# Query products of the head over 128 tokens at once instead of two tiles of 64

## The chip, the cores and the metric

The kernel runs on one core of a Trainium2 chip. The metric is the device time of one execution in microseconds (us), lower is better. Five engines work beside each other, each on its own list of instructions in order: TensorE (PE; the profile shows its weight loads as a row of their own, PEld), VectorE (DVE), ScalarE (ACT), GpSimd (POOL), and SyncE (SP), which here only issues DMAs.

## The reference

Two blocks follow each other. The first is a linear attention with a feature map of degree two: with `a = x S1^T` and `b = x S2^T` (8 values each), a token's 64 features are all products `a_i b_j`.

```python
q_p, k_p = phi(q), phi(k)                  # (b, h, s, 64)
kv  = einsum('bhsf,bhsd->bhfd', k_p, v)
z   = sum(k_p, axis=2)
num = einsum('bhsf,bhfd->bhsd', q_p, kv)
den = einsum('bhsf,bhf->bhs', q_p, z)[..., None] + 1e-6
x   = (num / den)                          # -> (4352, 128)
h   = x @ w_in                             # 128 -> 2048
out = where(h > 0, h, exp(min(h, 0)) - 1) @ w_out
```

q, k and v are (4, 4, 1088, 32) (batches, heads, tokens, width), in fp32. S1, S2 and the two weights arrive as 64-bit floats and are rounded to fp32 on the chip. All products are in fp32.

## The kernel before, in words

**Tiles.** A batch has 17 half tiles of 64 tokens (`NT`). The four heads of 32 make 128 partitions: `qT[b]` is (128, 17, 64), heads and widths down, half tiles and tokens along. All 68 half tiles are cut into 9 groups of 8 (512 tokens; the last has 4). `half_tile(g, k)` gives batch and half tile of the k-th of group g.

**Stages.** The head, up to about 15.6 us, computes the keys' features of batch 0 and from them `kv` and `z`, and then the queries of groups 0 and 1. After it the second block runs over the steps (group, pair of 128 columns of `w_in`): `mm1` makes `h`, ScalarE and VectorE apply the activation, `mm2` multiplies by `w_out`. For groups from 2 on a scheme with seven products instead of eight takes the place of `mm2`. Attention of later batches and groups is put between these steps.

**Order.** Nothing is scheduled by a planner: the order of calls in the code (lines 952 to 1006 for the head, then the loop of line 1107) is each engine's order of work. Waits on data are semaphores.

**TensorE tiles.** A product may use a part of the array's columns: `tile_position=(0, 64 * u)` puts a stationary operand of 64 columns in the left or right half, and two such products can stand side by side; 32 columns make four. The profile prints this form as 128*64 or 128*32, and the full array as 128*128. An fp32 product is recorded as two weight loads and two matmuls (a transpose as one of each).

**The steps that the change touches**, in the order of TensorE's list:

- `Z_first` (line 472): `z_tile` sums products of the keys' values over the tokens into `zps`; ScalarE copies the result to `zl` (line 441).
- `q1_first` (line 511): queries of group 0 times `Sab` (both sketches, 64 columns), into `abqp`. The queries are the stationary operand, in eight tiles of 64 tokens. ScalarE copies to `abq` (line 520).
- `Z` (line 444): `SXh` stationary, `zl` moving (32 columns), into columns 96 to 127 of `zps`, in two tiles of 64 for batch 0. `quarters` (line 254) cuts the stationary operand into tiles. VectorE masks the result into the third part of `SW` (`Z_out`, line 450): sketch and z folded into one matrix over the widths. Later batches call `Z` too, with the width that `width[0]` holds, and aren't touched.
- `keep_warm(1, 96, 64)` (line 261): products of ones that nothing reads, 96 columns in two tiles of 64.
- `q1z_first` (line 523): queries of group 0 times the z part of `SW` (32 columns), into `zqp`. VectorE multiplies it with `abq` into `pw` (line 603), sums (`den`, 608), takes the reciprocal (609), scales `a` (`an`, 611) and forms the 64 features per head (`qp`, 624, in two halves). Two weight roundings (`RA`, line 101) are put between.
- `KA(0)` (line 428) and `KS_first` (481): `kv` of batch 0 and its transpose `kvS`.
- `q4_early(0)` (line 636): eight transposes of `qp`; ScalarE copies to `qpT` (637).
- `q1_second` (line 532): queries of group 1 times all of `SW` (96 columns), into `abwp`. ScalarE copies to `abw` (541). It also waits for VectorE's transpose of the second part of `qT` (281).
- `q5_early(0)` (line 643): `kvS` times `qpT`, into `xps`; ScalarE copies to `xg` (649). With it the first `mm1` starts (`h`, line 257).

Of the kernel before, what the change touches and what calls it, by code (L numbers as in the profile page):

```python
# [27 lines left out]
def kernel(  # L28
# [21 lines left out]
    nc = tc.nc  # L50
    B, H, S, D = q.shape
    R = S1.shape[0]
    P = 128
# [19 lines left out]
    qT = [const.tile([FD, NT, 64], F32, name=f"qT{b}") for b in range(2)] * 2  # L73
# [180 lines left out]
    def quarters(dst, lhs, rhs, tile=None, **kw):  # L254
        tile = tile or width[0]
        for c in range(0, P, tile):
            nc.tensor.matmul(dst[c:c + tile], lhs[:, c:c + tile], rhs, skip_group_check=True,  # L257
                             tile_position=(0, c), **kw)


    def keep_warm(n, cols=256, tile=P):
        ones = nc.const_aps.tensor(1.0, [P, 256], F32)
        for i in range(n):
            for c in range(0, P, tile):
                nc.tensor.matmul(idle[c:c + tile, :cols], ones[:, :tile], ones[:, :cols], skip_group_check=True,  # L265
                                 tile_position=(0, c))
# [17 lines left out]
    SXh = const.tile([P, FD], F32, name="SXh")  # L284
# [10 lines left out]
    Sab = const.tile([FD, H, 2 * R], F32, name="Sab")  # L295
    SW = const.tile([FD, H, 3, R], F32, name="SW")
# [109 lines left out]
    def KO_first(t0, t1):  # L406
        half, o = divmod(t0, 5)
        n = t1 - t0
        a_ = kf_ps[half][:, 64 * o:64 * (o + n)].rearrange("p (m x r) -> p m x r", x=2, r=R)[:, :, 1, :]
        b_ = feats[0][:, 0, t0:t1].rearrange("p t h r -> p (t h) r")  # L410
        nc.vector.tensor_mul(feats[0, half][:, o:o + n].rearrange("p t h i j -> p (t h) i j"),
                             _ap(a_, list(a_.ap[1:]) + [[0, R]]), _ap(b_, [[R, n * H], [0, R], [1, R]]))
# [30 lines left out]

    def Z(b, ps, zl):

        quarters(ps[:, 96:128], SXh[:], zl[:], None if b else 64)

    def Z_out(b, ps):
        z = wzs[b] = SW[:, :, 2, :] if b == 0 else work.tile([FD, H, R], F32, name="wz", tag="wz")[:]
# [22 lines left out]
    def Z_first():  # L472
        ps = psum.tile([P, 512], F32, name="zps", tag="h", bufs=4)
        for i in range(KT):
            z_tile(0, ps, i)
        return ps, ZC(0, ps)
# [21 lines left out]
    def half_tile(g, k):  # L498
        return divmod(8 * g + k, NT)
# [11 lines left out]
    def q1_first():  # L511
        p = psum.tile([P, 512], F32, name="abqp", tag="aux")
        for i in range(4):
            for u in range(2):
                b, t = half_tile(0, 2 * i + u)
                nc.tensor.matmul(p[64 * u:64 * u + 64, i * 64:i * 64 + 64], qT[b][:, t, :],
                                 Sab[:].rearrange("p h y -> p (h y)"),
                                 skip_group_check=True, tile_position=(0, 64 * u))
        abw[0] = work.tile([P, H * 4, 2 * R], F32, name="abq", tag="abq", bufs=1)
        nc.scalar.copy(abw[0][:].rearrange("p (h t) y -> p h t y", h=H),  # L520
                       p[:, :256].rearrange("p (t h y) -> p h t y", t=4, h=H))

    def q1z_first():
        p = psum.tile([P, 512], F32, name="zqp", tag="h", bufs=4)
        for i in range(4):
            for u in range(2):
                b, t = half_tile(0, 2 * i + u)
                nc.tensor.matmul(p[64 * u:64 * u + 64, i * 32:i * 32 + 32].rearrange("p (h r) -> p h r", h=H),
                                 qT[b][:, t, :], SW[:, :, 2, :], skip_group_check=True, tile_position=(0, 64 * u))
        return p[:, :128].rearrange("p (t h r) -> p h t r", t=4, h=H)  # L530

    def q1_second():
        p = psum.tile([P, 512], F32, name="abwp", tag="h", bufs=4)
        for i in range(4):
            for u in range(2):
                b, t = half_tile(1, 2 * i + u)
                nc.tensor.matmul(p[64 * u:64 * u + 64, i * 96:i * 96 + 96], qT[b][:, t, :],
                                 SW[:].rearrange("p h x r -> p (h x r)"), skip_group_check=True,
                                 tile_position=(0, 64 * u))
        abw[1] = work.tile([P, H * 4, 3 * R], F32, name="abw1", tag="abq1", bufs=1)  # L540
        nc.scalar.copy(abw[1][:].rearrange("p (h t) y -> p h t y", h=H),
                       p[:, :384].rearrange("p (t h y) -> p h t y", t=4, h=H))
# [412 lines left out]
    transp(qT, "q", 0, 0, 8)  # L955
    zps, zl = Z_first()
    q1_first()
    KO_pool()
    KO_first(4, 5)
    KO_first(5, 7)  # L960
    Z(0, zps, zl)
    Z_out(0, zps)
    KO_first(7, KT)
    keep_warm(1, 96, 64)
    zq = q1z_first()
    q2_den(0, zq, lambda: RA(0))
    q2_out(0, 2, lambda: RA(1))
# [8 lines left out]
    RE(0)  # L976
    RE(1)
    q1_second()
    q5_early(0)
    keep_warm(1, 192, width[0])  # L980
# [62 lines left out]
    def turn(b):  # L1043
        Z(b, kv_ps[b], zls.pop(b))
        KV(b, kv_ps[b])
# [157 lines left out]
```

## Time and profile before

| | |
|---|---|
| median of 3 runs | 265.75 us (265.44 to 265.97) |
| profiled execution | 265.08 us, its span 263.3 us |
| PE busy | 257.8 us (98%), 4127 matmuls |
| PEld busy | 160.5 us (61%), 4127 loads |
| DVE, ACT, POOL busy | 188.2, 184.5, 168.2 us |
| granted TensorE clock | 1.0 (the mean over the span) |
| loads and matmuls of `abqp`, `zqp`, `abwp` | 16 each |
| loads and matmuls of `zps` in `Z` | 4 |

The span is the part of the execution that the trace covers. A row of the timeline has start and duration in us, engine, line, operation, output<-inputs, the form of the tile and the number of instructions merged into the row. Its duration runs from the start of the first to the end of the last. A matmul's record is longer than the time for which it holds the array, since matmuls are pipelined: the distance of two starts says more of the pace than one record's length.

### The profile page before, as it was taken

To read this page: it belongs to the slowest core of one execution; us is meant where nothing else is said; L and a number is where in the kernel's file an instruction comes from. 1 tells how busy PE (TensorE), PEld (TensorE's weight loads), DVE (VectorE), ACT (ScalarE), POOL (GpSimd) and SP (SyncE) were. 2 spreads that over 40 slices of the span, in tenths; PEclk is the share of its full clock that TensorE was granted. 3 is DMA by queue.
4 is the path that set the end of the run, shared out by engine and by line. 5 is a ranking of instruction groups with operands and counts; after the bars stand their busy time and mean duration, and the time that the engine had idled before them with its cause. 6 is when DMAs were issued, how large, how long until landed. Compare 5 with 4: busy or idle time off the path is not lost.

```text
span 263.3 us, 9739 instructions
## 1 busy us (share of the span) xinstructions
PE 257.8 (98%) x4127; PEld 160.5 (61%) x4127; DVE 188.2 (71%) x349; ACT 184.5 (70%) x356; POOL 168.2 (64%) x251
## 2 busy tenths in 40 slices
PE   8899999999999999999999999999999999999994
PEld 7652334354346756667666666665666666667994
DVE  6899999997969997996477676644446445674651
ACT  2479978677567656775587777776777777777793
POOL 4400009105477996798869799888688888998300
PEclk9999999999999999999999999999999999999999
DMA  5997099020011110000100110011001100110011
GB/s 176 339 349 209 2 277 230 1 72 18 2 24 26 26 20 2 2 4 17 31 3 0 29 18 0 2 19 25 3 2 21 23 4 0 18 20 8 2 30 32
DMA packets 26442, 13.73 MB, mean 52 GB/s; under 512 B 19328, under 2 KB 24576, under 8 KB 26400
## 3 DMA queue, kind: packets, MB, share of 16 engines
q1 hardware_dynamic: 25968, 12.76, 18.9%
q8 instruction: 32, 0.52, 0.9%
q10 hardware_dynamic: 368, 0.30, 0.3%
q0 software_dynamic: 64, 0.07, 0.1%
q14 instruction: 10, 0.08, 0.1%
HBM read 10.88 MB, written 2.23 MB: 50 GB/s over the span
## 4 chain that ended last, share of the span: by engine, by line
PE 96%; POOL 1%; DVE 1%; ACT 1%; issue 0%
PE h L257 44%; PE pb L792 16%; PE pa L792 13%; PE o L257 5%; PE pb L768 4%; PE ol L257 3%; PE idle L265 1%; PE kv L428 1%; PE h L686 1%; PE qps L686 1%; POOL kp L324 1%; PE kfps L360 1%; PE qps L576 1%; PE qtp L636 1%; PE kv L257 1%; PE abp L341 1%
## 5 line engine op out<-in xcount | busy, mean ns | idle before, releaser
L257 PE MATMUL h<-xg,W 128*32 128x512 f32 (+3 forms) x904 | 130.7, 539 | 0.4 <-ACT xg L649 0.4
L875 DVE SCALAR_TENSOR_TENSOR gg<-e,h 128x512 f32<-128x512 f32 x128 | 85.6, 683 | 54.1 <-ACT e L869 50.6
L867 ACT ACTIVATE e<-h 128x512 f32<-128x512 f32 x128 | 75.5, 590 | 45.6 <-PE h L257 42.9
L869 ACT ACTIVATE e<-e 128x512 f32<-128x512 f32 x128 | 80.9, 632 | 3.8
L257 PEld LDWEIGHTS h<-xg,W 128*32 128x32 f32 (+1 forms) x904 | 42.6, 122 | 43.2 <-issue 34.9
L754 POOL TENSOR_TENSOR tt<-gg 128x256 f32<-128x256 f32 x50 | 37.0, 741 | 16.4 <-DVE gg L875 16.1
L751 POOL TENSOR_TENSOR tt<-gg 128x256 f32<-128x256 f32 x50 | 36.7, 734 | 5.5 <-DVE gg L875 5.1
L755 POOL TENSOR_TENSOR tt<-tt,gg 128x256 f32<-128x256 f32 x50 | 37.5, 750 | 3.9
L756 POOL TENSOR_TENSOR tt<-gg,tt 128x256 f32<-128x256 f32 x50 | 37.2, 744 | 3.9
L792 PEld LDWEIGHTS pa<-gg,W 128*64 128x64 f32 (+1 forms) x496 | 23.8, 125 | 23.5 <-issue 22.9
L792 PE MATMUL pa<-gg,W 128*64 128x128 f32 (+1 forms) x496 | 30.5, 274 | 0.0
L792 PE MATMUL pb<-tt,SS 128*64 128x128 f32 (+1 forms) x480 | 29.5, 273 | 0.0
L792 PEld LDWEIGHTS pb<-tt,SS 128*64 128x64 f32 (+1 forms) x480 | 22.6, 126 | 0.0
L792 PE MATMUL pa<-tt,SS 128*32 128x128 f32 (+1 forms) x288 | 21.0, 273 | 0.0
L133 POOL TENSOR_TENSOR raw<-raw,tiny 128x512 f32<-128x512 f32 x1 | 1.0, 1044 | 29.4 <-DVE raw L128 29.4
L792 PE MATMUL pb<-tt,W 128*64 128x128 f32 (+1 forms) x256 | 19.8, 273 | 0.0
L792 PE MATMUL pb<-gg,SS 128*64 128x128 f32 (+1 forms) x256 | 19.8, 273 | 0.0
L257 PE MATMUL o<-gg,W 128*32 128x512 f32 x128 | 15.3, 594 | 0.0
L792 PEld LDWEIGHTS pa<-tt,SS 128*32 128x32 f32 (+1 forms) x288 | 13.6, 124 | 0.0
L792 PEld LDWEIGHTS pb<-gg,SS 128*64 128x64 f32 (+1 forms) x256 | 12.7, 125 | 0.0
L792 PEld LDWEIGHTS pb<-tt,W 128*64 128x64 f32 (+1 forms) x256 | 12.6, 125 | 0.0
L768 PE MATMUL pb<-gg,W 128*32 128x256 f32 x192 | 11.5, 380 | 0.0
(163 smaller groups left out, 279.5 us busy)
## 6 DMA issues: line engine op xcount, KB each, us to landing
raw<-in_moe_w_in_dram SPq DMA_DIRECT2D x8, 256.0 KB, 6.6
raw<-in_moe_w_out_dram SPq DMA_DIRECT2D x8, 256.0 KB, 6.4
hd_k<-in_k_dram SPq DMA_DIRECT2D x3, 544.0 KB, 7.3
hd_q<-in_q_dram SPq DMA_DIRECT2D x3, 544.0 KB, 7.9
out_dram<-ob SPq DMA_DIRECT2D x88, 16.0 KB, 1.5
v<-in_v_dram SPq DMA_DIRECT2D x4, 288.0 KB, 6.8
v<-in_v_dram SPq DMA_DIRECT2D x4, 256.0 KB, 8.3
hd_k<-in_k_dram SPq DMA_DIRECT2D x1, 288.0 KB, 3.3
```

The lines of the kernel that those rows point to most:

```text
L257: nc.tensor.matmul(dst[c:c + tile], lhs[:, c:c + tile], rhs, skip_group_check=True, tile_position=(0, c), **kw)
L265: nc.tensor.matmul(idle[c:c + tile, :cols], ones[:, :tile], ones[:, :cols], skip_group_check=True, tile_position=(0, c))
L686: nc.tensor.matmul(ps[w][s * r:s * r + s, 64 * k:64 * (k + m)], lhs, qpT[g, i][rows, o + 2 * k:o + 2 * (k + m), f, :], start=(f == 0 and j ...
L751: nc.gpsimd.tensor_tensor(t[:, 0], b12, b11, op=SUB)
L754: nc.gpsimd.tensor_tensor(t[:, 2], b22, b12, op=SUB)
L755: nc.gpsimd.tensor_tensor(t[:, 1], t[:, 2], b11, op=ADD)
L756: nc.gpsimd.tensor_tensor(t[:, 3], b21, t[:, 1], op=SUB)
L768: nc.tensor.matmul(acc[1][0][r:r + width[0], 256 * hi:256 * hi + 256], lhs[:, w:w + width[0]], gg[:, c, 256 * u:256 * u + 256], start=(cp ...
L792: nc.tensor.matmul(bank[r:r + width[0], P * col:P * col + P], lhs[:, w:w + width[0]], rhs[:, u], start=(first and i in ((0,) if g == 1 els ...
L867: nc.scalar.activation(e, hs[g, cp][c][:, :n], RELU, scale=-1.0)
L869: nc.scalar.activation(e, e, EXP, scale=-1.0)
L875: nc.vector.scalar_tensor_tensor(gs[g, cp][:, c, :n], es[g, cp][:, c, :n], -1.0, hs[g, cp][c][:, :n], op0=ADD, op1=MAX)
```

## The change

`q1_first`, `q1z_first` and `q1_second` take two neighbouring half tiles at once as a stationary operand of 128 columns, four products each instead of eight. Output places are the same: token 64 u + s of the pair is row 64 u + s. `Z` of batch 0 and the `keep_warm` after it use the whole array instead of two tiles of 64. The columns that stream, the waits and the order of calls stay.

```diff
     def Z(b, ps, zl):
-        quarters(ps[:, 96:128], SXh[:], zl[:], None if b else 64)
+        quarters(ps[:, 96:128], SXh[:], zl[:], None if b else P)
...
     def q1_first():
         p = psum.tile([P, 512], F32, name="abqp", tag="aux")
         for i in range(4):
-            for u in range(2):
-                b, t = half_tile(0, 2 * i + u)
-                nc.tensor.matmul(p[64 * u:64 * u + 64, i * 64:i * 64 + 64], qT[b][:, t, :],
-                                 Sab[:].rearrange("p h y -> p (h y)"),
-                                 skip_group_check=True, tile_position=(0, 64 * u))
+            b, t = half_tile(0, 2 * i)
+            nc.tensor.matmul(p[:, i * 64:i * 64 + 64], qT[b][:, t:t + 2, :].rearrange("p t y -> p (t y)"),
+                             Sab[:].rearrange("p h y -> p (h y)"), skip_group_check=True)
...
     def q1z_first():
         p = psum.tile([P, 512], F32, name="zqp", tag="h", bufs=4)
         for i in range(4):
-            for u in range(2):
-                b, t = half_tile(0, 2 * i + u)
-                nc.tensor.matmul(p[64 * u:64 * u + 64, i * 32:i * 32 + 32].rearrange("p (h r) -> p h r", h=H),
-                                 qT[b][:, t, :], SW[:, :, 2, :], skip_group_check=True, tile_position=(0, 64 * u))
+            b, t = half_tile(0, 2 * i)
+            nc.tensor.matmul(p[:, i * 32:i * 32 + 32].rearrange("p (h r) -> p h r", h=H),
+                             qT[b][:, t:t + 2, :].rearrange("p t y -> p (t y)"), SW[:, :, 2, :],
+                             skip_group_check=True)
...
     def q1_second():
         p = psum.tile([P, 512], F32, name="abwp", tag="h", bufs=4)
         for i in range(4):
-            for u in range(2):
-                b, t = half_tile(1, 2 * i + u)
-                nc.tensor.matmul(p[64 * u:64 * u + 64, i * 96:i * 96 + 96], qT[b][:, t, :],
-                                 SW[:].rearrange("p h x r -> p (h x r)"), skip_group_check=True,
-                                 tile_position=(0, 64 * u))
+            b, t = half_tile(1, 2 * i)
+            nc.tensor.matmul(p[:, i * 96:i * 96 + 96], qT[b][:, t:t + 2, :].rearrange("p t y -> p (t y)"),
+                             SW[:].rearrange("p h x r -> p (h x r)"), skip_group_check=True)
...
-    keep_warm(1, 96, 64)
+    keep_warm(1, 96)
```

## The prediction

> **What bounds the kernel now.** I read the page first, for the engine that carries the end: its busy line and the head line of its chain.
>
> ```profile
> PE 257.8 (98%) x4127; PEld 160.5 (61%) x4127; DVE 188.2 (71%) x349; ACT 184.5 (70%) x356; POOL 168.2 (64%) x251
> ...
> PE 96%; POOL 1%; DVE 1%; ACT 1%; issue 0%
> ```
>
> TensorE is the bound almost throughout. The question is whether a delay early in the program is still there at the end, so I cut the span where the first product of the second block, `h`, starts (15.58 us).
>
> ```profile
> core 0: us, PE busy (x) PEld busy (x) DVE busy (x) ACT busy (x) POOL busy (x), PEclk, DMA share, GB/s
> ...
> 15.58:24.00 8.42, 8.42 (x104) 3.59 (x108) 8.04 (x22) 7.20 (x15) 0.00 (x0) 1.00 1.07 305
> 24.00:260.00 236.00, 235.90 (x3802) 146.78 (x3794) 167.72 (x290) 170.31 (x326) 162.09 (x224) 1.00 0.13 29
> ```
>
> From 15.58 us PE is busy 8.42 of 8.42 and 235.90 of 236.00 us. The view of waits restricted to PE has no entry after 16 us. So there is no hole in which a late start could be recovered: what delays `h` at 15.58 us delays the end by as much.
>
> Everything edited runs before that. The timeline of 7.4 to 9.7 us (start, duration, both in us; the bracket is idle time and what ended it):
>
> ```profile
> 7.70 0.55 PEld L516 LDWEIGHTS abqp<-Sab,qT 128*64 128x64 f32 x16
> 7.70 0.69 PE L516 MATMUL abqp<-Sab,qT 128*64 128x64 f32 x16
> 7.84 0.19 ACT L441 COPY zl<-zps 128x32 f32<-128x32 f32 x1 [0.39 <-PE zps L419]
> ...
> 8.16 0.20 PEld L257 LDWEIGHTS zps<-zl,SXh 128*64 128x64 f32 x4
> 8.22 0.26 PE L257 MATMUL zps<-zl,SXh 128*64 128x32 f32 x4
> ...
> 8.60 0.19 DVE L450 TENSOR_TENSOR SW<-zps,bmask 128x32 f32<-128x32 f32 x1 [0.42 <-PE zps L257]
> 8.70 0.68 DVE L411 TENSOR_TENSOR kp<-abp,abk 128x512 f32<-128x512 f32 x1
> 8.84 0.55 PEld L528 LDWEIGHTS zqp<-SW,qT 128*64 128x64 f32 x16 [0.36 <-DVE SW L450]
> 8.84 0.66 PE L528 MATMUL zqp<-SW,qT 128*64 128x32 f32 x16 [0.17 <-DVE SW L450]
> ...
> 9.62 0.29 DVE L603 TENSOR_TENSOR pw<-abq,zqp 128x128 f32<-128x128 f32 x1 [0.23 <-PE zqp L528]
> ```
>
> This is one chain of waits. `zl` is ready at 8.03, but Z's product `zps` stands behind `abqp` in PE's order and loads only at 8.16; VectorE sat idle 0.42 us for it, PE 0.36 us for `SW`, VectorE 0.23 us for `zqp`. After `pw` VectorE works without a gap (`den`, its reciprocal, `an`, `qp`) to 12.51, and PE's second transpose of `qp` waits for that. The page's chain names POOL's copies before `den` (they end at 10.0); but `den` at 10.07 only follows the instruction before it on VectorE, so I take `pw` as the real step. Next, the timeline of 10 to 24 us:
>
> ```profile
> 13.24 0.69 PEld L537 LDWEIGHTS abwp<-SW,qT 128*64 128x64 f32 x16 [0.21 <-DVE qT L281]
> 13.25 0.88 PE L537 MATMUL abwp<-SW,qT 128*64 128x96 f32 x16
> ...
> 14.06 0.66 PE L643 MATMUL xps<-qpT,kvS 64*32 64x256 f32 x16
> ...
> 14.81 0.65 ACT L649 COPY xg<-xps 128x256 f32<-128x256 f32 x2 [0.15 <-PE xps L643]
> ...
> 15.58 2.79 PE L257 MATMUL h<-xg,W 128*32 128x256 f32 x40 [0.39 <-ACT xg L649]
> ```
>
> `abwp` stands between the transposes and `xps`; `xps` follows it at once (its other input, `qpT`, was ready at 13.31 + 0.59 = 13.90), then `xg`, then `h`. All three query products and Z are thus on the path.
>
> **What the Trainium skill says.** "TensorE: Matmul & The Clock Gate", section LDWEIGHTS: a load of the stationary operand costs about its number of columns / 1.2 in ns. The trace agrees: `zqp` and `abqp` have loads of 64 columns and both take 0.55 us for 16 loads, although `zqp` streams 32 columns per matmul and `abqp` 64; so the loads set the pace. A round of two loads is (0.55 - 0.14)/7 = 58.5 ns, against 64/1.2 = 53. "TensorEngine Tiling (Array Packing)", Key Properties: different tiles load and multiply in parallel. The trace agrees: the two 64-column tiles share one 58.5 ns round. The first page's section on row/col tiling says that loads overlap running matmuls only where the row group differs. The trace disagrees at 11.19 us: two full-width passes of 256 columns take 0.60 us with 0.382 for one, so they start 0.218 us apart, which is their streaming (the rate of `h`: 512 columns in 1.72/4 = 0.43 us, 1.19 per ns) with the second load hidden. I go with the trace.
>
> **The missing price: a 128-column load.** The loads by width (min/median/max in ns), first of tile `zps`, then of tile `idle` between 11.1 and 11.6 us:
>
> ```profile
> L419 PEld LDWEIGHTS zps<-abk x18: 106/109/113, 7.1 to 7.6; 128*32 128x32 f32 x18
> ...
> L257 PEld LDWEIGHTS zps<-zl,SXh x4: 133/137/138, 8.2 to 8.2; 128*64 128x64 f32 x4
> ```
>
> ```profile
> L265 PEld LDWEIGHTS idle<-const-float32-1.0 x2: 192/218/245, 11.0 to 11.2; 128*128 128x128 f32 x2
> L265 PE MATMUL idle<-const-float32-1.0 x2: 382/382/382, 11.2 to 11.4; 128*128 128x256 f32 x2
> ```
>
> 109, 137, 192 ns for 32, 64, 128 columns: 28 ns for the first 32 more and 55 for 64 more, so 0.86 ns a column on a fixed part of some 80. A load of 128 columns then holds the path for 128 x 0.86 = 110 ns. The skill's formula gives 107, scaling the 58.5 ns round gives 117; I take 110. From below: the 128-column transposes of `qp` have loads of 140 ns, the same as for 64 columns, which would mean 58 ns. From above: if loads did not overlap, the streaming time adds to it.
>
> **The change part by part.** Each product is two passes (two loads, two matmuls) per tile. Before, a round is two tiles side by side in one pass; after, one 128-column load and matmul, bounded by the larger of 110 ns and the streaming (64, 32, 96 columns: 54, 27, 81 ns), so 110 everywhere.
>
> 1. `q1_first` (`abqp`): 8 rounds of 58.5 = 0.47 us become 8 of 110 = 0.88: +0.41. Nothing else covers it: `zl` has waited since 8.03, so Z's load moves from 8.16 to about 8.57. ScalarE's copy `abq` comes later too, but is used only by `pw`.
> 2. Z (`zps`): last matmul of `abqp` to last of Z is 0.09 us in the rows (8.16 to 8.25); two loads of 110 make 0.22: +0.13. `SW` moves from 8.60 to 9.14. Behind it on VectorE waits the `kp` product of 0.68 us, which then ends near 9.93, still before `pw`.
> 3. `keep_warm`: two passes instead of four, some 0.3 us inside PE's wait for `SW` (0.36 us before, as long after): 0. Uncovered it would cost about 0.1.
> 4. `q1z_first` (`zqp`): 8 rounds again, 0.47 to 0.88: +0.41. `pw` moves from 9.62 to about 10.57: +0.95 in all. Everything behind `pw` on VectorE (two weight roundings and the transpose of `qT` too) and behind `zqp` on PE (the `kv` products, which wait for nothing else: POOL's `kp` is done at 9.07) moves along; the transposes of `qp` and the start of `abwp`, which waits for VectorE's `qT`, by +0.95.
> 5. `q1_second` (`abwp`): first load to last matmul was 13.24 to 13.88 = 0.64 us (rounds of 82, bound by 96 columns); 8 loads of 110 are 0.88: +0.24, straight into `xps`, whose `qpT` has only 0.1 us of slack and moved by 0.95 itself. The change of tiling between transpose and `abwp` goes; before, the wait for `qT` stood there, so it gains 0.
>
> No DMA is moved and no wait added; SP's and POOL's queues are passed by nothing. Sum: 0.41 + 0.13 + 0.41 + 0.24 = 1.19, so +1.2 us at `h`, unrecovered to the end. Against the profiled execution, 265.08 with its span of 263.3 (1.8 us around it), that is a span of 264.5 and 266.3 us; the median of the runs is 0.67 above that execution, so 265.75 + 1.2 = 266.95 us. With 107 and 117 ns a load (26 loads in the sum) it is 1.1 and 1.4.
>
> **Rivals.**
> A, the wide load costs what the 64-column one costs. For: the transposes' loads of 140 ns. Against: those are another mode of load, and the plain 128-column row has 192. Then rounds stay at 58.5 and 82 ns: 265.75, no change.
> B, wide loads do not hide under matmuls. For: the skill's sentence. Against: the 0.218 us above. Rounds of 164, 137, 137, 191 ns (`abqp`, Z, `zqp`, `abwp`): +0.84, +0.18, +0.63, +0.89 = 2.5, so 268.3 us.
> C, the end on the other side, faster: PE is paced by the number of instructions, 29 ns a load-matmul pair, in `abqp`, Z and `zqp`. 36 pairs become 18: 18 x 29 = 0.52 saved, 265.2. It decides if the round stays near 29 ns with one pair in it. Against: the 32-column tiles' loads of `zps` come 8 in 0.16 us with 0.109 for one, 7 ns apart, far below 29.
> D, half of the delay is recovered before the end, for example because the edited path was not the last of two: +0.6, 266.35. For: the chain names POOL near 10.0. Against: PE's missing waits after 16 us.
>
> **How the numbers follow.** Forecast 0.78, A 0.08, B 0.08, C 0.02, D 0.04. A measurement of this kernel can tell about 0.2%, 0.53 us. The forecast's own range is 266.6 to 267.4: 1.1 to 1.4, with 0.25 for the spread of the runs shown. The range stretches down to D and up towards a partly hidden load: 266.3 to 267.8. Slower: forecast, B and most of D, 0.88; same: A and the rest of D, 0.10; faster: C, 0.02.
>
> **What would show it.** Step 1: eight `abqp` loads in 0.19 + 7 x 0.11 = 0.96 us, of some 190 ns each; Z's first load near 8.57. Step 2: `SW` near 9.14. Step 4: `pw` near 10.57. Step 5: `abwp` over 0.95 us of loads, `h` near 16.8. Then the same stages from there, 1.2 us late. The prediction is wrong if loads of 128 columns come 58 ns apart (A), 140 or more (B), or if `h` is 1.2 us late and the end is not.

## The result and the profile after

The changed kernel takes 266.50 us (median of 7 runs, 266.11 to 266.64) against 265.68 us (7 runs, 265.24 to 265.97): 1.0033 times the time of before, 95% interval 1.0021 to 1.0045. That is +0.82 us by the medians. The forecast was +1.2, so the direction is right and the forecast nearly half too large: 266.50 us lies between rival D's 266.35 and the forecast's 266.95, nearer to D. The profiled execution of after took 266.64 us with a span of 264.7.

The page of after, busy line and head of the chain:

```profile
PE 259.5 (98%) x4099; PEld 162.3 (61%) x4099; DVE 188.3 (71%) x349; ACT 184.5 (70%) x356; POOL 168.2 (64%) x251
...
PE 97%; DVE 1%; issue 0%; ACT 0%; DVEq 0%
```

Loads and matmuls fell by 28 each: eight in each of the three query products, two in Z, two in `keep_warm`. PE is busy 1.7 us longer with fewer instructions. The same two stretches as before, counted from where `h` now starts (16.89 us):

```profile
core 0: us, PE busy (x) PEld busy (x) DVE busy (x) ACT busy (x) POOL busy (x), PEclk, DMA share, GB/s
16.89:25.31 8.42, 8.42 (x104) 3.60 (x108) 8.04 (x22) 7.34 (x16) 0.00 (x0) 1.00 0.94 268
25.31:261.31 236.00, 235.88 (x3802) 146.76 (x3794) 167.82 (x290) 170.38 (x326) 162.16 (x224) 1.00 0.13 28
```

8.42 us and 236 us hold the same work as before. From the first load of `h` on, PE's loads are 1.31 us later than before, constant within 0.03 us to the last load: nothing is recovered.

The timeline of after, the rows that answer to those shown of before:

```profile
8.20 0.97 PEld L515 LDWEIGHTS abqp<-Sab,qT 128*128 128x128 f32 x8
8.21 1.10 PE L515 MATMUL abqp<-Sab,qT 128*128 128x64 f32 x8
8.34 0.19 ACT L441 COPY zl<-zps 128x32 f32<-128x32 f32 x1 [0.39 <-PE zps L419]
...
9.09 0.30 PEld L257 LDWEIGHTS zps<-zl,SXh 128*128 128x128 f32 x2
...
9.54 0.19 DVE L450 TENSOR_TENSOR SW<-zps,bmask 128x32 f32<-128x32 f32 x1 [0.86 <-PE zps L257]
...
9.79 0.97 PEld L525 LDWEIGHTS zqp<-SW,qT 128*128 128x128 f32 x8 [0.17 <-DVE SW L450]
...
10.98 0.29 DVE L599 TENSOR_TENSOR pw<-abq,zqp 128x128 f32<-128x128 f32 x1 [0.64 <-PE zqp L525]
...
14.57 0.97 PEld L534 LDWEIGHTS abwp<-SW,qT 128*128 128x128 f32 x8 [0.20 <-DVE qT L281]
...
15.63 0.18 PEld L639 LDWEIGHTS xps<-qpT,kvS 64*32 64x32 f32 x16
...
16.38 0.65 ACT L645 COPY xg<-xps 128x256 f32<-128x256 f32 x2 [0.17 <-PE xps L639]
...
16.86 1.91 PEld L257 LDWEIGHTS h<-xg,W 128*32 128x32 f32 x40 [0.48 <-ACT xg L645]
```

Eight wide loads take 0.97 us in all three products, whether 64, 32 or 96 columns stream: (0.97 - 0.19)/7 = 111 ns a load.

One thing must be taken out before the two profiles are compared. `abqp` starts at 8.20 instead of 7.70 us, although nothing before it was edited. The cause lies in the products before it: PE's groups by form up to some 7 us, first of before, then of after (busy us, mean ns):

```profile
L341 PE MATMUL abp<-Sab,kT 128*64 128x64 f32 x36 | 2.0, 228 | 0.0
...
L288 PE MATMUL SXps<-Sx,idr 128*128 128x128 f32 x2 | 0.5, 316 | 0.0
```

```profile
L341 PE MATMUL abp<-Sab,kT 128*64 128x64 f32 x36 | 2.3, 272 | 0.0
...
L288 PE MATMUL SXps<-Sx,idr 128*128 128x128 f32 x2 | 0.8, 491 | 0.0
```

The same two matmuls of `SXps` have a mean of 491 instead of 316 ns: in this execution the full TensorE clock was granted at 6.70 us after the start, in the other at 4.58. This belongs to the execution and not to the kernel: the experiments' profiles have it between 3.6 and 7.0 us, and one with the head of before up to `abqp` (the run with three times `abwp`) has it at 6.98 and `abqp` at 8.36. The span's +1.43 us is then 0.50 before `abqp`, 0.81 between `abqp` and `h`, and 0.12 after `h` (0.14 behind the last product, less 0.02 ahead of it). The 0.81 is the change, and agrees with the medians. So below I use distances inside one trace (first load to first load, `SW` and `pw` by their starts, `h` by its first matmul; the traces hold these to the ns).

| distance, us | before | after | difference | forecast |
|---|---|---|---|---|
| `abqp` to Z | 0.461 | 0.888 | +0.43 | +0.41 |
| Z to `SW` | 0.434 | 0.453 | +0.02 | +0.13 |
| `SW` to `pw` | 1.022 | 1.432 | +0.41 | +0.41 |
| `pw` to `abwp` | 3.627 | 3.589 | -0.04 | 0 |
| `abwp` to `xps` | 0.811 | 1.062 | +0.25 | +0.24 |
| `abwp` to `h` | 2.333 | 2.323 | -0.01 | +0.24 |
| `abqp` to `h` | 7.877 | 8.685 | +0.81 | +1.19 |

`xps` is late by all that was forecast, `h` isn't. Something else must have held `h` back before.

### The profile page after: what moved, and what is told of

The parts are those of the page before. It is cut to its first block, busy times and chain, and to the rows that moved or that the text cites. A ratio compares the mean times of both kernels' runs of the same rounds, so it can differ in the third digit from the quotient of the medians.

```text
span 264.7 us, 9682 instructions
## 1 busy us (share of the span) xinstructions
PE 259.5 (98%) x4099; PEld 162.3 (61%) x4099; DVE 188.3 (71%) x349; ACT 184.5 (70%) x356; POOL 168.2 (64%) x251
## 4 chain that ended last, share of the span: by engine, by line
PE 97%; DVE 1%; issue 0%; ACT 0%; DVEq 0%
PE h L257 44%; PE pb L788 16%; PE pa L788 13%; PE o L257 5%; PE pb L764 4%; PE ol L257 3%; PE idle L265 1%; PE kv L428 1%; PE h L682 1%; PE qps L682 1%; PE abp L341 1%; PE kfps L360 1%; PE qps L572 1%; PE qtp L632 1%; PE kv L257 1%; PE xps L639 0%
```

## The theory after the result, and its rivals

`h` needs two things: `xg`, and the rounded first block of `W` from VectorE, whose last step is line 136. The rows of before, then of after (each `xg` row is the first of its two copies):

```profile
14.81 0.37 ACT L649 COPY xg<-xps 128x256 f32<-128x256 f32 x1 [0.15 <-PE xps L643]
15.01 0.76 DVE L136 SCALAR_TENSOR_TENSOR W<-raw,W 128x256 f32<-128x256 f32 x2
```

```profile
16.32 0.76 DVE L136 SCALAR_TENSOR_TENSOR W<-raw,W 128x256 f32<-128x256 f32 x2
...
16.38 0.37 ACT L645 COPY xg<-xps 128x256 f32<-128x256 f32 x1 [0.17 <-PE xps L639]
```

Of the two instructions for `W` (0.42 us each) the first makes block 0: in before it ends at 15.43. The first products of `h` use only the half of `xg` that the first of two copies makes: it ends at 14.81 + 0.37 = 15.18. So `W` came last, by 0.25 us, and `h` followed 0.15 us after it. The bracket `<-ACT xg` names the second copy, which ended at 15.46 but isn't waited for: in after it ends at 17.03, when `h` has already started (16.89). In after, `W` ends at 16.74 and `xg`'s first half at 16.75: `abwp`'s delay used up that difference, no more.

The new theory: the path is `abqp`, Z, `zqp`, `pw`, VectorE's gapless list from `pw` to `W`, `h`. The rival is the prediction as it was (`abwp`, `xps`, `xg`, `h`), with the missing 0.24 lost somewhere else.

The traces hold one more sign. The wait for VectorE's `W` is an instruction of its own ahead of `h`'s first load. In before it ends at 15.52 us, and the load follows at 15.55: nothing else was left to wait for.

## Experiments

Times are medians with the ratio to runs of the kernel before on the same chip. The distances come from each run's profile.

**One part alone: `abwp`.**

```diff
 # the kernel before, with q1_second of the kernel after
-        for u in range(2): ... qT[b][:, t, :] ... tile_position=(0, 64 * u)
+        ... qT[b][:, t:t + 2, :] ...
```

> The kernel before with q1_second alone changed (abwp at 128 columns). Step 5 of the prediction: abwp's loads take 0.97 instead of 0.69 us, xps follows 0.25 us later, and h with it: first load of abwp to first h matmul grows from 2.33 to 2.57 us, the time by 0.24. New theory (h waits for VectorE's rounding of W, line 136, which ends at 15.43 us in the profile before, while the first half of xg is ready at 15.18): xps is 0.25 us later too, but abwp to h stays at 2.33 to 2.38 us and the time within 0.05 us of before.

265.49 against 265.39 us, 1.0002 (0.9994 to 1.0010). `abwp` to `xps` 1.062, `abwp` to `h` 2.321 us. Timeline:

```profile
13.23 0.97 PEld L536 LDWEIGHTS abwp<-SW,qT 128*128 128x128 f32 x8 [0.21 <-DVE qT L281]
...
14.29 0.18 PEld L641 LDWEIGHTS xps<-qpT,kvS 64*32 64x32 f32 x16
...
14.98 0.76 DVE L136 SCALAR_TENSOR_TENSOR W<-raw,W 128x256 f32<-128x256 f32 x2
15.04 0.65 ACT L647 COPY xg<-xps 128x256 f32<-128x256 f32 x2 [0.17 <-PE xps L641]
15.52 1.91 PEld L257 LDWEIGHTS h<-xg,W 128*32 128x32 f32 x40 [0.48 <-ACT xg L647]
```

The loads cost what was said and `xps` is late by it, but `h` keeps its distance from `W`. Step 5's size is right and its place isn't on the path.

**All parts but `abwp`.** The kernel after, with `q1_second` of the kernel before.

> The kernel after with q1_second alone undone. Prediction: 0.24 us faster than after, some 0.57 us slower than before; first load of abqp to first h matmul 8.44 us (7.88 before, 8.69 after). New theory: as slow as after, some 0.8 us slower than before, with abqp to h at 8.65 to 8.70 us.

266.54 against 265.39 us, 1.0034 (1.0022 to 1.0047); `abqp` to `h` 8.691 us, where the prediction asks for 8.44. `abwp` to `xps` is back at 0.811 us, `abwp` to `h` stays at 2.329. Undoing the step wins nothing.

**Z alone.**

```diff
-        quarters(ps[:, 96:128], SXh[:], zl[:], None if b else 64)
+        quarters(ps[:, 96:128], SXh[:], zl[:], None if b else P)
...
-    keep_warm(1, 96, 64)
+    keep_warm(1, 96)
```

> The kernel before with Z and the keep_warm after it alone changed. Prediction: Z's two wide loads add 0.13 us; Z's first load to SW grows from 0.44 to 0.57 us, time +0.13. New theory (the wide form frees VectorE's SW of a second wait, worth 0.09 us): 0.45 us, time +0.01.

265.71 against 265.39 us, 1.0011 (1.0003 to 1.0019); `abqp` to `h` 8.048 us (+0.17). Z to `SW` is 0.447 us, as the new theory says, but both missed what comes before it:

```profile
7.82 0.55 PEld L516 LDWEIGHTS abqp<-Sab,qT 128*64 128x64 f32 x16
...
8.44 0.30 PEld L257 LDWEIGHTS zps<-zl,SXh 128*128 128x128 f32 x2
...
8.88 0.19 DVE L450 TENSOR_TENSOR SW<-zps,bmask 128x32 f32<-128x32 f32 x1 [0.59 <-PE zps L257]
```

`abqp` to Z grew from 0.461 to 0.615 us with the same 16 loads. Alone, the wide Z puts a change of tile form between `abqp` (128*64) and Z (128*128), which neither kernel has there. The Trainium skill ("TensorEngine Tiling (Array Packing)", Key Properties) says that a change of tiling mode drains TensorE; this one came with 0.154 us. That the change of form is the cause is argued from the row, not tried apart. In the whole change it costs nothing, because `abqp`, Z and `zqp` change together.

**`zqp` alone.** The kernel before, with `q1z_first` of the kernel after.

> The kernel before with q1z_first alone changed. Both theories: eight loads of 112 ns instead of eight rounds of 58, SW's start to pw's grows from 1.02 to 1.44 us, h and the time by 0.42 us. If VectorE had slack after pw, less.

265.84 against 265.39 us, 1.0017 (1.0010 to 1.0024); `SW` to `pw` 1.430 us, `abqp` to `h` 8.243 (+0.37). As said, less some 0.04 us that VectorE's list gains between `pw` and `abwp` (3.588 instead of 3.627, as in after). The two attempts at a faster version below have 3.59 too, with `zqp` as in before, so the wide form need not be the cause; it stays open.

**Taking work off VectorE ahead of `W`.** The kernel leaves out one step of the rounding, 0.44 us on VectorE, so it computes another `h`.

```diff
-            for f in (round_s, round_m, round_d):
+            for f in (round_s, round_d):
```

> The kernel before without the masking of the high words of the first two blocks of w_in on VectorE (line 120, 0.44 us; this part of the rounding is left out, so h of these blocks is another). Prediction, with h waiting for xg: no change. New theory, with h waiting for VectorE's W: h comes 0.25 us earlier, until xg ends the wait; abwp's first load to h 2.08 us instead of 2.33, time 0.25 us below before if PE keeps its pace afterwards.

265.22 against 265.52 us, 0.9988 (0.9979 to 0.9996), and `abwp` to `h` is 1.990 us. Less work on VectorE moves `h` and the end, with PE's products unchanged:

```profile
13.42 0.69 PEld L537 LDWEIGHTS abwp<-SW,qT 128*64 128x64 f32 x16 [0.21 <-DVE qT L281]
...
14.58 0.76 DVE L136 SCALAR_TENSOR_TENSOR W<-raw,W 128x256 f32<-128x256 f32 x2
14.99 0.65 ACT L649 COPY xg<-xps 128x256 f32<-128x256 f32 x2 [0.15 <-PE xps L643]
15.41 1.88 PEld L257 LDWEIGHTS h<-xg,W 128*32 128x32 f32 x40 [0.43 <-ACT xg L649]
```

Here `W` is ready at 15.01 and `h` follows `xg`: its first half ends 0.05 us before `h`'s first matmul, where in before it was 0.395. So the slack of `xg` was 0.34 us. The 0.25 of the expectation left out that `h` starts 0.15 us after `W` when it waits for that, and 0.05 us after `xg` here: the wait for `W`, an instruction of its own, is over at 15.10, and the load waits for `xg` itself.

All eleven profiles fall in these two groups: `h` starts 0.146 or 0.147 us after `W` in eight (before, after, the single parts, all but `abwp` and the two attempts below), and 0.052 or 0.053 us after the first half of `xg` in the other three (this run, the next and three times `abwp`).

The same edit in the kernel after:

> The kernel after without the same masking (the same part of the rounding left out). Prediction: no change against after. New theory: here xg's first half (16.75 us) and W (16.74) end together, so at most 0.06 us is won: abwp to h 2.27 to 2.32 us, and the time stays 0.76 to 0.82 us above before. Taken with the run of the kernel before without the mask, the whole change then costs 1.0 to 1.07 us.

266.17 against 265.52 us, 1.0028 (1.0016 to 1.0039); `abwp` to `h` 2.245 us, 0.08 less than after and more than the 0.06 expected at most: so much of the 0.34 us was left when `abwp` had taken 0.25. Against the run before this one, `abwp` to `h` is 0.255 us longer: with the mask's work gone `xg` ends the wait in both kernels, and step 5 reaches `h` in full. By the medians the change then costs 266.17 - 265.22 = 0.95 us, expected were 1.0 to 1.07; the 0.13 more than with the mask isn't clear of the spread of these runs. In this profile the granted clock was 0.50 from 10.66 to 14.07 us and the `kv` products were slower, which is why only the distance behind them is used.

**More of `abwp`.**

```diff
-        for i in range(4):
+        for i in 3 * list(range(4)):
```

> The kernel before with abwp's products made three times over (16 more rounds of 82.7 ns, 1.32 us, the same result). Prediction: abwp to h grows by all of it, from 2.33 to 3.65 us, time +1.32. New theory: 0.25 us of it lies in the slack of xg, so 3.40 us, time +1.07.

266.98 against 265.52 us, 1.0049 (1.0036 to 1.0062). The time alone doesn't decide. The distances do:

```profile
13.91 2.12 PEld L537 LDWEIGHTS abwp<-SW,qT 128*64 128x64 f32 x48 [0.21 <-DVE qT L281]
...
15.66 0.76 DVE L136 SCALAR_TENSOR_TENSOR W<-raw,W 128x256 f32<-128x256 f32 x2
16.15 0.18 PEld L643 LDWEIGHTS xps<-qpT,kvS 64*32 64x32 f32 x16
...
17.33 0.37 PEld L257 LDWEIGHTS h<-xg,W 128*32 128x32 f32 x12 [0.43 <-ACT xg L649]
```

`xps` comes 1.425 us later (0.1 more than 16 rounds of 82.7 ns), `h` 1.08 us: 0.34 us lay in the slack, the same figure as above. That `abwp` to `h` came out at 3.415 us, near the 3.40 expected, is luck: the products cost 0.1 us more and the slack held 0.1 us more. Past the slack, `abwp` does set `h`.

**Two attempts at a faster version.** If `W` holds `h`, block 0 should be rounded first.

```diff
-            for f in (round_s, round_m, round_d):
+            for f in (round_s, round_m):
...
     RC_2()
+    RD(0)
     RE(0)
-    RE(1)
+    RD(1)
+    round_w(round_e, 1, True)
```

> A version meant to be faster than before: the third step of the rounding (line 128) for block 0 alone first, then its last step, so that W of block 0 is ready 0.26 us earlier; the last step of block 1 moves from VectorE to POOL. Prediction: no change. New theory: h 0.2 to 0.25 us earlier, VectorE 0.17 us less work by the next activation, so 0.1 to 0.25 us faster than before.

265.50 against 265.52 us, 1.0003 (0.9994 to 1.0011). `abwp` to `h` is 2.055 us, 0.28 less, as the theory says. The lead isn't kept:

```profile
15.57 0.74 DVE L101 TENSOR_SCALAR W<-raw 128x256 uint32<-128x256 uint32 x1
...
16.23 0.75 POOL L134 TENSOR_TENSOR W<-raw,W 128x256 f32<-128x256 f32 x1
...
17.03 0.16 PEld L257 LDWEIGHTS h<-xg,W 128*32 128x32 f32 x8 [0.32 <-POOL W L134]
```

The loads for block 1 wait for POOL, whose two instructions take 0.62 and 0.75 us, but that costs little: counted from `abqp`, PE is 0.32 us ahead of before at `h` and still 0.27 at the first transpose of group 1's `qp`. At the fifth transpose it is 0.14, since VectorE ends `qp` 0.15 us later than before. Its rounding step (line 101) took 0.74 us instead of 0.29, while POOL worked on block 1; that POOL's work slowed it is argued, not shown. At the last product 0.05 us is left.

The second attempt keeps these steps on VectorE and moves half of a later product to POOL.

```diff
+    RD(0)
     RE(0)
+    RD(1)
     RE(1)
...
-            nc.vector.tensor_mul(qp[g][:, h], ...
+            (nc.gpsimd if g == 1 and i else nc.vector).tensor_mul(qp[g][:, h], ...
```

> Second attempt at a version faster than before: the third rounding step is split as in the first attempt, but both last steps stay on VectorE; VectorE is relieved by POOL making the second half of group 1's qp (line 624, 0.69 us on VectorE, an estimated 1.0 us on POOL). If VectorE's rounding of W alone holds h back, and VectorE's load before the next activation is what gave it back in the first attempt: h 0.3 us earlier (abwp's first load to h near 2.05 us instead of 2.33) and still 0.3 us earlier after 22 us, time 0.2 to 0.3 us below before. If something else takes it back after h: time as before.

265.38 against 265.46 us, 0.9990 (0.9974 to 1.0007): not told apart from before. `abwp` to `h` is 2.060 us, but the product took 1.51 us on POOL instead of the 1.0 that I had estimated (POOL's 1.96 us for a product of 128x1024 in before would give 0.98), and the transposes waited:

```profile
17.34 1.51 POOL L624 TENSOR_TENSOR qp<-an,abw 128x512 f32<-128x512 f32 x1 [8.23 <-DVE an L611]
...
18.90 0.42 PEld L636 LDWEIGHTS qtp<-ident,qp 128*128 128x128 f32 x4 [0.45 <-POOL qp L624]
```

PE's lead of 0.31 us at `h`, counted from `abqp`, is a lag of 0.12 us from the fifth transpose on. Neither version beats the kernel before: in both the lead turned into a wait for `qp` some 3 us behind the start of `h`.

## Why the prediction was right, and where it failed

- **The price of a wide load** was right: 110 ns forecast, 111 measured in three products. Rivals A (58 ns) and B (137 to 191 ns) are out, and so is C: half as many pairs did not make any group shorter. The rate from three load durations (0.86 ns a column) carried it, and so did the choice of the trace over the sentence on overlapping loads in the Trainium skill ("TensorE: Matmul & The Clock Gate", section on row/col tiling): in `abqp`, matmuls of 64 columns cost nothing on top of the loads. The same section also names loads into a background weight buffer as ones that can run ahead, which the prediction didn't mention.
- **Steps 1 and 4** were right: +0.43 and +0.41 for +0.41 each.
- **Step 2** was mis-sized: +0.13 forecast, +0.02 measured. The loads do cost most of their part: Z's first load to the end of its last matmul record grew by 0.10 us. But before, a wait instruction of its own stood ahead of `SW` on VectorE (two semaphores to wait for), and with the single wide product it's gone, so the waits did not all stay as the change was described: `SW` starts 0.04 us after Z's last matmul record instead of 0.12. Z alone gives about the same distance from Z to `SW` (0.447 us). All profiles with the wide Z have the 0.04, all others the 0.12; the wait was not tried apart from the tile form.
- **Step 5 failed**, in the words "straight into `xps`" and, ahead of it, "then `xg`, then `h`": `xps` is 0.25 us late, `h` isn't. The bracket on `h`'s row was taken at its word. What ended that wait was the rounding of `W` on VectorE, with 0.34 us of slack for `xg`. The run with `abwp` alone and the one with all but `abwp` show that `h` doesn't wait for the step, and the runs with less VectorE work and with three times the product show the same 0.34 us from both sides.
- **No recovery after `h`** was right: `h` is 1.31 us late and the last product 1.29. Rival D named the right kind of cause, an edited path that isn't the last of two, but placed it near 10.0 us, where `pw` held. Ahead of `h` it cost the forecast 0.25 of the 0.38 us that never came; 0.11 is step 2, and the rest the 0.04 between `pw` and `abwp` less small gains. That the measured time still lies within the prediction's wide range (266.3 to 267.8 us) owes something to luck: the narrower one began at 266.6, and the wide one reached down to D for a reason that the prediction took to be unlikely.
- A reading without effect: `abq` is not used by `pw` alone; `an` and `qp` read it too, later.
- The sum as it should have stood: 0.43 + 0.02 + 0.41 - 0.04 + 0 = 0.82, less 0.01 = 0.81 us.

## What to carry to other kernels

The products here, with 32 to 96 streamed columns, were paced by the loads of their stationary operand in the wide form: two tiles of 64 columns side by side loaded in 58 ns what one of 128 took 111 ns for, so fewer, wider instructions were slower. Before a delay is added up to the end, each wait on the path needs its second input checked: put the end times of all that an instruction reads beside its start, and don't take the bracket's name alone: here it named a copy that wasn't waited for and that ended 0.03 us after the true cause. Where the time at which the full clock is granted moves between executions, compare distances inside one trace.

## What was not expected of the hardware

- The time at which the full TensorE clock was granted lay between 3.6 and 7.0 us in eleven profiles of nearly the same head, and `abqp`'s first load between 7.69 and 8.36 us. With the clock granted by 4.6 us it started at 7.69 to 7.75, with 5.3 and 5.9 at 7.82 and 7.87, with 6.4 to 7.0 at 8.18 to 8.36. One profile (the changed kernel without the mask) doesn't fit, 3.83 and 7.99: there VectorE waited 0.87 us for the DMA of q. That this makes the spread of the runs (265.2 to 266.0 us in one series of the kernel before, 265.2 to 267.6 in another) isn't shown.
- A change of tile form between `abqp` and Z came with 0.15 us more between their first loads (Z alone; the cause is argued).
- Where the wait that ended last is an instruction of its own, the work began 0.08 to 0.09 us later than where the wait belongs to the working instruction: 0.12 against 0.04 us for `SW`, 0.147 against 0.053 for `h`.
- POOL took 1.51 us for a product of 128x512 with repeated operands that VectorE did in 0.69.
